# The shift of a DiT block's modulation, computed by four 128x32 column tiles of TensorE in place of 81 narrow matmuls

## The chip, the core and the metric

The kernel runs on one core of one Trainium2 chip. The metric is the device time of one execution in microseconds (us). "Before" is the kernel without the change, "after" the kernel with it. The engines are TensorE (PE; its weight loads, PEld, are listed apart), VectorE (DVE), ScalarE (ACT), GpSimd (POOL) and SyncE (SP), which issues most of the DMAs.

## The reference

The first half of a DiT block with adaptive layer norm: two samples of 256 tokens with 1152 features, one attention head over all features, all inputs in bf16.

```python
B, N, D = 2, 256, 1152
mod = (silu(c) @ w_mod).reshape(B, 6, 1, D)
shift_a, scale_a, gate_a, shift_m, scale_m, gate_m = [mod[:, i] for i in range(6)]
h = layernorm(x) * (1 + scale_a) + shift_a          # eps 1e-5, no affine
qkv = h @ wqkv
q, k, v = qkv[..., :D], qkv[..., D:2*D], qkv[..., 2*D:]
p = softmax(einsum('bqd,bkd->bqk', q, k) * D ** -0.5)
a = einsum('bqk,bkd->bqd', p, v) @ wo
return x + gate_a * a
```

Only the first three of the six parts of `mod` are used: the shift, the scale and the gate of the attention.

## The kernel before

The 512 tokens (T) of both samples lie side by side in the free dimension; the 1152 features are KT = 9 blocks of P = 128 partitions. x is normalised, turned so that features lie on the partitions (`xnT`), and multiplied by 1 + scale. Everything runs in one pass, in this order:

1. *Load.* SP issues the loads in a written order: x, the scale columns of w_mod (`wS`), K's columns of wqkv (`wK`), the shift columns of w_mod (`wH`, five DMAs), then Q's and V's columns in chunks of 384 (`wqv`), the gate columns (`wG`) and wo (`wO`). The rows of w_mod are dealt out so that partition p holds the rows 9p to 9p + 8; so one step kk of a product with w_mod takes one of the nine rows of every partition.
2. *K without the shift.* K is computed from `hTs`, the normalised tokens times 1 + scale, without the shift and before the 1/std of each token is applied. A shift of h adds to the scores of a query one number for all keys, which softmax drops. K's feature blocks 0 to 5 (`accs`) accumulate while x and the weights arrive; the first three k of blocks 6 and 7 are kept in `early`. What is left of blocks 6 and 7 (six matmuls each, k = 3 to 8) is computed later by `k_block` and added to `early` by VectorE; these are the two "early blocks". Block 8 (`k_block(8, ps, 0)`) is nine matmuls.
3. *1/std.* `rstd_bc`, the 1/std of each token on all partitions, is copied out of `spread_ps`, and VectorE multiplies it into the nine blocks of `xnT`.
4. *Shift.* `shift_block(kk)` accumulates the shift in `psH`: for each of the nine feature blocks j it loads the 128x128 block of `wH` as the stationary operand and lets silu(c) stream past it. silu(c) of the two samples is repeated 27 times to NR = 54 columns (`scT_rep`). So one step kk is nine weight loads and nine matmuls of 54 columns, and nine steps are 81. Four steps run before early block 6, one after it, four after early block 7. Then VectorE copies two of the 54 columns of each block to `sh`, a table of 128 partitions x 9 blocks x 2 samples.
5. *hT.* `modulated(i)` makes the full h from `xnT`, `s1p` (1 + scale) and `sh`, 18 instructions of 128x256: two of every three on VectorE, the third on ScalarE. K's block 8 runs on TensorE meanwhile.
6. *Q.* Nine feature blocks f, each nine matmuls over k of `hT` with 512 columns; ScalarE copies each block out to `qkT`.
7. *Scores, softmax, V, attention, output.* VectorE makes the gate in 18 steps (`gate_step`) between other work and GpSimd sums it over the partitions (`gate_bc`). The output projection, gate and residual end the kernel.

The order of each engine's instructions is the order in which the program issues them: helpers (`ten`, `vec`, `sca`, `gps`, `spq`) record every instruction, and `pin` ties each to the one before it on its engine. All of these instructions therefore carry one line in the profile, L74, and are told apart by the names of their tiles. PSUM has eight banks here: six in the pool `psum` (tag "mm"), one each in `psum_a` and `psum_b`. `evac(1, ...)` is a copy on ScalarE.

Of the kernel before, what the change touches and what calls it, by code (L numbers as in the profile page):

```python
# [10 lines left out]
F32 = mybir.dt.float32  # L11
# [5 lines left out]
def kernel(  # L17
# [10 lines left out]
    P = 128  # L28
    B, N, D = x.shape
    T = B * N  # L30
    KT = D // P
    TT = T // P
    NQ = N // P
    CW = 384
# [5 lines left out]
    NEARLY = 2  # L40
# [3 lines left out]
    NR = 54  # L44
# [7 lines left out]
    const = ctx.enter_context(tc.tile_pool(name="const", bufs=1))  # L52
# [4 lines left out]
    psum = ctx.enter_context(tc.tile_pool(name="psum", bufs=6, space=PSUM))  # L57
    psum_a = ctx.enter_context(tc.tile_pool(name="psum_a", bufs=1, space=PSUM))
# [22 lines left out]
    vec = _Rec(nc.vector, dve_seq)  # L81
    sca = _Rec(nc.scalar, act_seq)
    ten = _Rec(nc.tensor, pe_seq)
# [12 lines left out]
    def tok(b):  # L96
        return slice(b * N, (b + 1) * N)
# [4 lines left out]
        out=ident, in_=ident, compare_op=ALU.not_equal, fill=1.0, base=0,  # L102
# [14 lines left out]
        out=pick, in_=pick, compare_op=ALU.is_ge, fill=0.0, base=0,  # L117
# [3 lines left out]
        out=pick, in_=pick, compare_op=ALU.is_ge, fill=0.0, base=NT - 1,  # L121
# [12 lines left out]
    chunks_w = [wpool.tile([P, KT, CW], BF16, tag=f"wchunk{i}", name="wqv") for i in range(2 * NCH)]  # L134
    wmpool = ctx.enter_context(tc.tile_pool(name="wmpool", bufs=1))
    wS = wmpool.tile([P, KT, D], BF16, tag="wS")
    wH = wmpool.tile([P, KT, D], BF16, tag="wH")
# [63 lines left out]
    def sc_rhs(kk):  # L201
        return scT_rep[:, kk].rearrange("p r b -> p (r b)")
# [5 lines left out]
    hT = act.tile([P, KT, T], BF16)  # L208
# [62 lines left out]
    def rstd_spread():  # L271
        ps = psum_a.tile([P, TT, P], F32, tag="pa", name="spread_ps")
        for t in range(TT):
# [3 lines left out]


    s1p = const.tile([P, KT, B], F32)
    sh = const.tile([P, KT, B], F32)  # L280
    hTs = act.tile([P, KT, T], BF16, tag="a3")
    qkT = act.tile([P, 2 * KT, T], BF16)
    early = const.tile([P, NEARLY, T], F32)
# [3 lines left out]
               rhs=ones_row[0:1, 0 : (KA - 1) * NR], start=True, stop=False, skip_group_check=True)  # L287
    psS0 = psum_b.tile([P, NR], F32, tag="pb")
    ten.matmul(psS0, lhsT=ones_bf[0:1, :], rhs=ones_row[0:1, 0:NR], start=True, stop=False,
               skip_group_check=True)  # L290
# [19 lines left out]
            for b in range(B):  # L310
                scaled(k, tok(b), s1p[:, k, b : b + 1])

    def shift_block(kk):
        for j in range(KT):
            ten.matmul(
                psH[:, j, :], lhsT=wH[:, kk, j * P : (j + 1) * P], rhs=sc_rhs(kk),
                start=(kk == 0 and j == 0), stop=(kk == KT - 1), skip_group_check=True,
            )

    def one(t):  # L320
# [26 lines left out]
    def k_block(f, ps, k0):  # L347
        for k in range(k0, KT):
            ten.matmul(
                ps, lhsT=wK[:, k, f * P : (f + 1) * P], rhs=hTs[:, k, :],  # L350
                start=(k == k0), stop=(k == KT - 1),
            )

    def evac(idx, out_ap, in_ap):
        if idx % 2 == 0:
            return vec.tensor_copy(out=out_ap, in_=in_ap)
        return sca.copy(out=out_ap, in_=in_ap)
# [100 lines left out]
        k_step(k)  # L458
    for f in range(NACC):
        evac(1, qkT[:, KT + f, :], accs[f])  # L460
    psH = psum_a.tile([P, KT, NR], F32, tag="pa")
    for kk in range(4):
        shift_block(kk)
    for i in range(NEARLY):
        pool, tag = (psum_b, "pb") if i == 0 else (psum, "mm")
        ps = pool.tile([P, T], F32, tag=tag, name="ps")
        k_block(NACC + i, ps, KA)
        vec.tensor_tensor(out=qkT[:, KT + NACC + i, :], in0=ps, in1=early[:, i, :], op=ALU.add)
        shift_block(4 + i)
    for kk in range(4 + NEARLY, KT):  # L470
        shift_block(kk)
    vec.tensor_copy(out=sh, in_=psH[:, :, 0:B])
    for f in range(NACC + NEARLY, KT):
        ps = psum.tile([P, T], F32, tag="mm")
        k_block(f, ps, 0)
# [32 lines left out]
        spq.dma_start(out=wO[:, k0 : k0 + 3, :], in_=wo_v[:, k0 : k0 + 3, :])  # L508


    for f in range(KT):
        wt, off = chunks_w[f * P // CW], f * P % CW
        ps = psum.tile([P, T], F32, tag="mm")
        for k in range(KT):
            ten.matmul(
                ps, lhsT=wt[:, k, off : off + P], rhs=hT[:, k, :],
                start=(k == 0), stop=(k == KT - 1),
            )
        evac(1, qkT[:, f, :], ps)


    s_tiles = []
    for b in range(B):
        s_ps = psum.tile([P, NQ, N], F32, tag="mm")
        for i in range(NQ):
            tq = b * NQ + i
            for k in range(KT):
                ten.matmul(
                    s_ps[:, i, :],
                    lhsT=qkT[:, k, tq * P : (tq + 1) * P],  # L530
                    rhs=qkT[:, KT + k, tok(b)],
                    start=(k == 0), stop=(k == KT - 1),
# [96 lines left out]
    for b in range(B):  # L629
        for gi, dv0 in enumerate(range(0, KT, 2)):  # L630
            ndv = min(2, KT - dv0)
            ps = psum.tile([P, 2, N], F32, tag="mm")
            for dd in range(ndv):
                dv = dv0 + dd
                for j in range(NQ):
                    ten.matmul(
                        ps[:, dd, :], lhsT=v_sb[:, b * NQ + j, dv * P : (dv + 1) * P], rhs=pT_sbs[b][:, j, :],
                        start=(j == 0), stop=(j == NQ - 1),
# [3 lines left out]
    for t in range(TT):  # L642
# [9 lines left out]
        for ci, (c0, w_) in enumerate(chunks):  # L652
# [3 lines left out]
            ps = psum.tile([P, w_], F32, tag="mm")  # L656
            if pregated:
                ten.matmul(ps, lhsT=ident, rhs=x_sb[:, t, cs], start=True, stop=False)
            for k in range(KT):
                ten.matmul(  # L660
                    ps, lhsT=attnT[:, k, t * P : (t + 1) * P],
                    rhs=(wo_last[:, k, c0 - (D - TAILW) : c0 - (D - TAILW) + w_] if pregated else wO[:, k, cs]),
                    start=(k == 0 and not pregated), stop=(k == KT - 1),
# [50 lines left out]
```

## Time and profile before

| | us |
|---|---|
| median of 3 runs | 98.16 (97.86 to 98.18) |
| the profiled execution, whole | 97.95 |
| the profiled execution, span from its first to its last instruction | 96.2 |
| TensorE busy | 91.2 (95% of the span) |
| VectorE busy | 70.6 (73%) |
| ScalarE busy | 33.5 (35%) |
| GpSimd busy | 21.4 (22%) |
| mean granted clock of TensorE | 0.996 of full speed |
| bytes moved by DMA | 21.31 MB |

All other times are positions in the span or durations of that one execution. A row of the timeline gives the start, the length, the engine, the line, the operation, "out<-in" by the program's names, the shape and how many instructions were merged into the row. A row of the groups gives the busy time, the mean length of one instruction in ns, and the idle time of the engine before them with what ended it. A matmul row's length runs from its start to the modelled end of its results; matmuls overlap, so a stream advances faster than one instruction's length tells. In the chain of waits a piece is the time that the chain spent at this work.

### The profile page before, as it was taken

The page shows a single profiled execution, that of the slowest core. Times are in us where ns is not written, and L with a number is a line of the kernel's source. Part 1 is how long each engine was busy: PE and PEld are TensorE (multiplying, and loading weights), DVE is VectorE, ACT ScalarE, POOL GpSimd, SP SyncE. Part 2 cuts the span into 40 slices and gives each one's busy share as a digit, 9 for nine tenths or more (in the row PEclk, how much of TensorE's full clock was granted, in tenths as well). Part 3 has the DMA queues.
Part 4 walks back from the last instruction along what each step waited for, and adds up shares of the span by engine and source line. Part 5 has one row for each costly group of instructions (what it writes and reads, how often), then busy time and mean ns, then how long its engine had stood idle before and what let it go on. Part 6 is the DMA issues. An engine that isn't in the chain of part 4 may idle for free.

```text
span 96.2 us, 1804 instructions
## 1 busy us (share of the span) xinstructions
PE 91.2 (95%) x715; PEld 55.5 (58%) x720; DVE 70.6 (73%) x139; ACT 33.5 (35%) x67; POOL 21.4 (22%) x26
## 2 busy tenths in 40 slices
PE   5998899999999999999999999999999999999970
PEld 1338698454566444444458755665568755665760
DVE  0488589132999999999982999990229577999880
ACT  5297667202560962432231445331115400000010
POOL 6600000710000000000000000008999980007000
PEclk9999999999999999999999999999999999999998
DMA  2999999999999999999999502200000000303221
GB/s 47 303 350 344 348 391 375 396 395 407 395 380 400 383 407 393 373 371 372 383 410 410 220 2 55 50 5 0 0 0 0 7 0 0 123 1 122 98 97 51
DMA packets 19015, 21.31 MB, mean 222 GB/s; under 512 B 2752, under 2 KB 13632, under 8 KB 19008
## 3 DMA queue, kind: packets, MB, share of 16 engines
q1 hardware_dynamic: 18592, 21.16, 61.4%
q10 hardware_dynamic: 416, 0.05, 0.4%
q8 instruction: 5, 0.08, 0.3%
q14 instruction: 2, 0.02, 0.0%
HBM read 19.76 MB, written 1.18 MB: 218 GB/s over the span
## 4 chain that ended last, share of the span: by engine, by line
PE 85%; DMA 9%; DVE 1%; SPq 1%; issue 1%; ACT 0%
PE ps L74 63%; PE acc L74 12%; DMA x_sb<-in_x_dram 4%; DMA wK<-in_wqkv_dram 4%; PE s_ps L74 4%; PE psH L74 2%; PE psE L74 1%; PE tp L74 1%; SPq L74 1%; PE psL L74 1%; DVE xnT L74 0%; PE spread_ps L74 0%; ACT o_sb L74 0%; DVE hTs L74 0%; DVE o_sb L74 0%
## 5 line engine op out<-in xcount | busy, mean ns | idle before, releaser
L74 POOL PARTITION_ALL_REDUCE gate_bc<-gacc x2 | 13.7, 6886 | 45.5 <-DVE gacc L74 45.5
L74 DVE SCALAR_TENSOR_TENSOR gacc<-wG,scT_f,gacc 128x1152 f32<-128x1152 bf16 x16 | 22.7, 1418 | 0.5
L74 PE MATMUL ps<-wqv,hT 128*128 128x384 bf16 x108 | 17.7, 326 | 0.0
L74 PE MATMUL ps<-hT,wqv 128*128 128x512 bf16 x80 | 17.6, 379 | 0.1
L74 PE MATMUL ps<-wO,attnT 128*128 128x384 bf16 (+1 forms) x108 | 17.0, 319 | 0.0
L74 PEld LDWEIGHTS <-attnT 128*128 128x128 bf16 x117 | 11.3, 98 | 6.3
L74 PEld LDWEIGHTS <-hT 128*128 128x128 bf16 x108 | 10.6, 98 | 6.9
L74 PE MATMUL acc<-hTs,wK 128*128 128x128 bf16 (+2 forms) x88 | 13.3, 292 | 0.8 <-DVE hTs L74 0.3
L74 PEld LDWEIGHTS <-wK 128*128 128x128 bf16 x123 | 9.9, 97 | 6.5 <-DMA wK<-in_wqkv_dram 0.7
L74 PEld LDWEIGHTS <-wqv 128*128 128x128 bf16 x81 | 7.8, 97 | 9.6 <-DVE hT L74 0.4
L74 ACT CAST qkT<-ps 128x512 bf16<-128x512 f32 x10 | 5.8, 583 | 10.9 <-PE ps L74 10.9
L74 DVE TENSOR_TENSOR ga<-ps,gate_bc 128x384 f32<-128x384 f32 (+1 forms) x12 | 6.5, 538 | 2.4 <-PE ps L74 2.4
L74 ACT CAST v_sb<-ps 128x384 bf16<-128x384 f32 x10 | 4.7, 476 | 9.8 <-PE ps L74 9.8
L74 DVE TENSOR_TENSOR o_sb<-ga,x_sb 128x384 bf16<-128x384 f32 (+1 forms) x12 | 7.0, 585 | 0.4
L74 DVE TENSOR_TENSOR xnT<-xnT,rstd_bc 128x512 bf16<-128x512 bf16 x9 | 5.5, 685 | 1.8 <-ACT rstd_bc L74 1.8
L74 PE MATMUL junk_ps<-junk_rhs 128*128 128x512 bf16 x13 | 5.7, 627 | 1.1 <-DVE junk_rhs L74 1.1
L74 ACT CAST o_sb<-ps 128x128 bf16<-128x128 f32 x1 | 0.3, 265 | 17.3 <-PE ps L74 17.3
L74 DVE BATCH_NORM_STATS2 stats<-x_sb 128x6 f32<-128x384 bf16 x6 | 3.1, 552 | 2.5 <-DMA x_sb<-in_x_dram 2.5
L74 PE MATMUL ps<-hTs,wK 128*128 128x512 bf16 x19 | 4.7, 378 | 0.1
L74 DVE CAST attnT<-ps 128x512 bf16<-128x512 f32 (+1 forms) x6 | 3.5, 603 | 1.7 <-PE ps L74 1.7
L74 DVE COPY xnT<-tp 128x384 bf16<-128x384 bf16 (+2 forms) x7 | 2.2, 347 | 3.3 <-PE tp L74 3.3
L74 DVE CAST v_sb<-ps 128x384 bf16<-128x384 f32 x2 | 1.1, 558 | 4.6 <-PE ps L74 4.6
(84 smaller groups left out, 91.8 us busy)
## 6 DMA issues: line engine op xcount, KB each, us to landing
wqv<-in_wqkv_dram SPq DMA_DIRECT2D x5, 864.0 KB, 10.1
wG<-in_w_mod_dram SPq DMA_DIRECT2D x3, 864.0 KB, 9.6
wO<-in_wo_dram SPq DMA_DIRECT2D x3, 864.0 KB, 8.5
wH<-in_w_mod_dram SPq DMA_DIRECT2D x4, 576.0 KB, 7.8
wS<-in_w_mod_dram SPq DMA_DIRECT2D x6, 288.0 KB, 6.0
wK<-in_wqkv_dram SPq DMA_DIRECT2D x6, 288.0 KB, 6.2
x_sb<-in_x_dram SPq DMA_DIRECT2D x4, 288.0 KB, 3.8
wqv<-in_wqkv_dram SPq DMA_DIRECT2D x3, 288.0 KB, 9.0
```

The lines of the kernel that those rows point to most:

```text
L74: r = fn(*a, **k)
```

## The change

- `shift_rows(kk)` takes the place of `shift_block(kk)`. Now silu(c) is the stationary operand, its first 32 columns (16 repeats of the two samples), and the row kk of `wH` moves. The array is used as four column tiles of 128x32 (`tile_position=(0, 32 * j)`): tile j gets of each of the nine feature blocks the 32 columns 32j to 32j + 31, so 288 moving columns, and writes the PSUM partitions 32j to 32j + 31. One step is four weight loads of 32 columns and four matmuls of 288; nine steps are 36.
- In `psH` the shift now lies with samples on the partitions (32 rows for each tile, only two of them different) and features in the free dimension. One VectorE `transpose`, which turns each 32x32 block by itself, writes it to `sh`; `sh` grows to 128 x 9 x 32, and its first two columns of each block are read as before.
- All nine steps stand in one piece after the two early blocks of K, ahead of K's block 8.
- Q's feature blocks 0 and 1 are computed side by side: for each k one matmul of each, into two PSUM tiles, and the two copies after both. The other seven blocks are as before.

```diff
-    sh = const.tile([P, KT, B], F32)
+    sh = const.tile([P, KT, 32], F32)
...
-    def shift_block(kk):
-        for j in range(KT):
+    def shift_rows(kk):
+        w4 = wH[:, kk, :].rearrange("p (f j c) -> p f j c", j=4, c=32)
+        for j in range(4):
             ten.matmul(
-                psH[:, j, :], lhsT=wH[:, kk, j * P : (j + 1) * P], rhs=sc_rhs(kk),
-                start=(kk == 0 and j == 0), stop=(kk == KT - 1), skip_group_check=True,
+                psH[32 * j : 32 * (j + 1), :, :], lhsT=sc_rhs(kk)[:, 0:32], rhs=w4[:, :, j, :],
+                start=(kk == 0), stop=(kk == KT - 1), skip_group_check=True, tile_position=(0, 32 * j),
             )
...
-    psH = psum_a.tile([P, KT, NR], F32, tag="pa")
-    for kk in range(4):
-        shift_block(kk)
     for i in range(NEARLY):
         pool, tag = (psum_b, "pb") if i == 0 else (psum, "mm")
         ps = pool.tile([P, T], F32, tag=tag, name="ps")
         k_block(NACC + i, ps, KA)
         vec.tensor_tensor(out=qkT[:, KT + NACC + i, :], in0=ps, in1=early[:, i, :], op=ALU.add)
-        shift_block(4 + i)
-    for kk in range(4 + NEARLY, KT):
-        shift_block(kk)
-    vec.tensor_copy(out=sh, in_=psH[:, :, 0:B])
+    psH = psum_a.tile([P, KT, 32], F32, tag="pa")
+    for kk in range(KT):
+        shift_rows(kk)
+    vec.transpose(out=sh.rearrange("p f r -> p (f r)"), in_=psH.rearrange("p f r -> p (f r)"))
     for f in range(NACC + NEARLY, KT):
         ps = psum.tile([P, T], F32, tag="mm")
         k_block(f, ps, 0)
...
-    for f in range(KT):
-        wt, off = chunks_w[f * P // CW], f * P % CW
-        ps = psum.tile([P, T], F32, tag="mm")
+    for fs in ((0, 1), *((f,) for f in range(2, KT))):
+        pss = [psum.tile([P, T], F32, tag="mm", name="ps") for _ in fs]
         for k in range(KT):
-            ten.matmul(
-                ps, lhsT=wt[:, k, off : off + P], rhs=hT[:, k, :],
-                start=(k == 0), stop=(k == KT - 1),
-            )
-        evac(1, qkT[:, f, :], ps)
+            for f, ps in zip(fs, pss):
+                wt, off = chunks_w[f * P // CW], f * P % CW
+                ten.matmul(
+                    ps, lhsT=wt[:, k, off : off + P], rhs=hT[:, k, :],
+                    start=(k == 0), stop=(k == KT - 1),
+                )
+        for f, ps in zip(fs, pss):
+            evac(1, qkT[:, f, :], ps)
```

## The prediction

> **What bounds the kernel now.** I read the page first, its busy shares and slices, to see which engine sets the pace.
>
> ```profile
> PE 91.2 (95%) x715; PEld 55.5 (58%) x720; DVE 70.6 (73%) x139; ACT 33.5 (35%) x67; POOL 21.4 (22%) x26
> PE   5998899999999999999999999999999999999970
> PEclk9999999999999999999999999999999999999998
> ```
>
> TensorE (PE) is busy 95% of the 96.2 us span at its full granted clock, with no thin slice between the first and the last 5 us. What it no longer does there can shorten the run; what others do counts only where TensorE waits for it. Next the chain of waits, at the stretch that the change touches.
>
> ```profile
> 23.41 2.70 PE acc L74 x12
> 26.10 0.91 PE psH L74 x36
> 27.01 0.06 issue
> 27.07 1.24 PE ps L74 x5
> 28.31 0.23 PE psH L74 x9
> 28.53 1.29 PE ps L74 x6
> 29.83 0.91 PE psH L74 x36
> 30.74 0.21 PE ps L74
> 30.96 0.05 issue
> 31.01 10.74 PE ps L74 x49
> ```
>
> The chain stays on TensorE: the shift (psH) stands on it with 36 + 9 + 36 = 81 matmuls and 0.91 + 0.23 + 0.91 = 2.05 us, 25.3 ns each. Then the timeline of the two engines that meet here, TensorE and VectorE (DVE).
>
> ```profile
> 25.94 1.07 PE L74 MATMUL psH<-scT_rep,wH 128*128 128x54 bf16 x36
> 32.52 7.72 PE L74 MATMUL ps<-hT,wqv 128*128 128x512 bf16 x35
> ...
> 24.06 5.51 DVE L74 TENSOR_TENSOR xnT<-xnT,rstd_bc 128x512 bf16<-128x512 bf16 x9 [1.77 <-ACT rstd_bc L74]
> 29.49 1.28 DVE L74 TENSOR_TENSOR qkT<-ps,early 128x512 bf16<-128x512 f32 x2
> 30.78 0.18 DVE L74 COPY sh<-psH 128x18 f32<-128x18 f32 x1
> 30.99 3.17 DVE L74 TENSOR_SCALAR hT<-xnT,s1p,sh 128x256 bf16<-128x256 bf16 x12
> ```
>
> Two things are to be seen. From the first shift matmul (25.94) to Q's first (32.52) lie 6.58 us: 81 of the shift and 21 of K with 512 columns at 0.216 us each (35 in 7.72: (7.72 - 0.379)/34 = 0.216), 4.53 + 2.05. No wait of TensorE is left in it. And VectorE has no gap from 24.06 to 34.1: its copy of sh starts at 30.78 because VectorE comes free then, as the last shift matmul ends. So VectorE is the second bound, right behind the first.
>
> **The change, part by part.** The durations come from the groups of instructions:
>
> ```profile
> L74 DVE TENSOR_TENSOR ga<-ps,gate_bc 128x288 f32<-128x288 f32 x2 | 0.9, 458 | 0.2 <-PE ps L74 0.2
> L74 PE MATMUL ps<-wO,attnT 128*128 128x288 bf16 x18 | 2.4, 286 | 0.0
> L74 PEld LDWEIGHTS <-wH 128*128 128x128 bf16 x81 | 2.5, 96 | 0.7
> L74 PE MATMUL turn_ps<-ident,parts 128*12 128x128 bf16 x1 | 0.2, 222 | 0.0
> ```
>
> *Removed:* 81 weight loads and 81 matmuls of 54 columns: -2.05 us of TensorE.
>
> *Added on TensorE:* 9 x 4 = 36 matmuls with a 32-column stationary and 9 x 32 = 288 moving columns each. What a stream pays per matmul: 0.216 us at 512 columns, 0.109 at 256 (36 of s_ps in 4.09 us: (4.09 - 0.272)/35), so 0.42 ns per column and 0.122 us at 288. A narrow stationary is no cheaper by itself: turn_ps, with 12 columns, took 222 ns where 36 full transposes of the same length average 219. So the price hangs on whether the four tiles of a step run side by side, which no row of before shows. Ends: side by side 9 x 0.122 = 1.10 us; one after another 36 x 0.122 = 4.41 us. I take side by side: the four are given separate 32-column tiles and write separate partitions, so nothing in the data orders them, and TensorE already keeps some seven of the shift's matmuls in flight (each lasts 185 ns, one starts every 25). The floor that the same row gives, 36 x 25.3 = 0.91 us, is below 1.10.
>
> To this come two changes between full array and tiles. Ends: nothing, or each time TensorE empties and loads weights anew, 286 - 122 = 164 ns of matmul after its last column plus 96 ns, 0.26 us; twice 0.52. The Trainium skill (TensorEngine Tiling (Array Packing), Key Properties) says that a change of tiling mode drains TensorE, which speaks for the upper end; no row here shows it, and by it the stage would take 1.10 + 0.52 = 1.62 us. I take 0.4 for both, nearer to the upper end, since the 25 ns at which whole-array weights follow one another are the pace of a pipe that stays full. Stage: S = 1.50 us, between 1.10 and 1.62.
>
> *Moved:* all of the shift comes after K's two early blocks. TensorE runs these 12 matmuls from 25.94 to 28.53, the shift until 28.53 + S = 30.03, K's last block (9 x 0.216 = 1.94) until 31.97. From TensorE's side Q could start at 30.47 + S = 31.97, against 32.52. The early blocks move up by up to 1.1 us, yet their two additions on VectorE stay where they are, since the nine products of xnT hold it until 29.5. PSUM is free: acc's first copies on ScalarE begin at 25.06, spread_ps was read by 24.02. No DMA and no queue of SP or GpSimd moves. w_mod's last rows are issued at 19.86 and take 8.9 us, so they land at 28.8; the last step needs them at 28.53 + 8 x 0.122 + a drain, 29.5 or later. Cover 0.7 us; gone, each late microsecond is one on TensorE.
>
> *VectorE:* the copy of 18 elements (177 ns) becomes a transpose of 288 fp32 columns from PSUM. No row has that operation. Ends: 0.22 us (the shortest copy of a transposed block, 128x128 bf16, 220 ns) and 0.76 us (two passes at the 1.05 ns per column between the PSUM reads of 256 and 512 fp32 columns, 424 and 692 ns, over their 156 ns of fixed cost). I take the row with the same size, type and source, 458 ns. VectorE comes free at 30.78, long after the shift's end at 30.03 + 0.16; behind the transpose queue the 12 hT instructions. The transpose ends at 31.24, hT starts at 31.28, its first k (two instructions, 0.60 us) is there at 31.88, and Q's first matmul may start some 0.05 later: 31.93.
>
> So Q starts at the later of 31.93 (VectorE) and 31.97 (TensorE): 31.97, or 0.55 us earlier. VectorE caps the gain: S = 1.10 would take 0.95 us off TensorE, but TensorE would then wait from 31.57 to 31.93. The two bounds meet at S = 1.46.
>
> *Q side by side:* the same 18 matmuls in another order, no price of its own. It covers hT's pace: its last k is ready 3.17 us after hT's start, 31.28 + 3.17 = 34.45. One block alone would want it at 31.97 + 8 x 0.216 = 33.70 and stall 0.75 us; the pair reaches it at 31.97 + 16 x 0.216 = 35.43. In between too: k = 3 needs six of VectorE's instructions, 5 x 0.257 + 0.34 = 1.63 us, so 32.91; the pair is there at 33.27. The pair's copies on ScalarE both come at its end, 2 x 0.58 us, while f = 2 takes 1.94.
>
> *After that* nothing takes the gain back: wqv's third chunk, issued at 31.09, lands 11.2 us later at 42.3 and is wanted at 44.2 - 0.55; VectorE's gates begin 0.3 us later but it idles 2.0 us before p_f; GpSimd has gate_bc's second half at 78.9, wanted at 83.
>
> **Sum.** -0.55 us: the profiled execution's 97.95 us (span 96.2) becomes 97.40. The median of the runs shown is 98.16, 0.21 above the profiled one; from it, 97.6.
>
> **Rivals.** *Rounds do not overlap.* The Trainium skill (TensorE: Matmul & The Clock Gate, Part 3) states that weight loads overlap matmuls in flight only where the row groups differ; column tiles use all rows. In before's trace it does not hold for whole-array weights: wH's loads start at 25.73 while K's matmuls run, with none lost. Should it hold for tiles, a step's weights wait until the matmuls of the step before have ended: 9 x (0.286 + 0.096) = 3.44 us in place of 2.05. Place: between the steps of the shift. TensorE binds (30.47 + 3.44 = 33.91 against 32.52): +1.4, 99.55 us, slower. It decides against the change from S = 2.05, that is from 0.11 us of exposed time per step above 1.10. For it: each step accumulates on the same 32 partitions as the one before, with other weights. Against: so do all of before's steps of psH, at 25 ns. Chance 0.12.
>
> *Only the loads are exposed.* The tiles overlap, but each step adds a load of 96 ns: 1.10 + 0.86 = 1.96, and with the changes of mode 2.0 to 2.5: 98.1 to 98.6, taken 98.3. Chance 0.15, split between no change and slower.
>
> *The tiles run one after another* (the change doesn't do what it says): S = 4.41, Q at 34.88, +2.36, 100.5. For it: turn_ps, where unused columns buy nothing. Chance 0.14.
>
> *The transpose is dear:* at 0.76 us hT starts at 31.58, Q at 32.23: 97.9; at 1.05 us the gain is nil, 98.2. Against: no VectorE row of up to 300 columns takes half of that. Chance 0.05, nearly all of it no change.
>
> **How the numbers follow.** The forecast case has the other 0.54. With S from 1.10 to 1.62 and the transpose from 0.22 to 0.76, Q starts between 31.69 and 32.23, so its own range is 97.3 to 97.9. About 0.3% (0.3 us) is what a measurement of this kernel can tell from no change; the case is faster by more in 0.51 of all and within it in 0.03. Faster 0.51; no change 0.03 + 0.08 + 0.05 = 0.16; slower 0.12 + 0.07 + 0.14 = 0.33. The range runs from 97.3 to 99.6, over the rounds that do not overlap; left out are the serial tiles (0.14) and some 0.05 below.
>
> **What would show it.** Right: psH's 36 matmuls in fours starting within a few tens of ns and a new four every 0.12 us; 28.53 to about 30.0 for the stage; the transpose at 30.8 behind the two additions, near 0.46 us; Q's first matmul near 31.95 and no gap in the pair. Wrong: psH's matmuls evenly 0.12 us apart (serial), or fours 0.2 to 0.4 us apart (loads or rounds exposed); a transpose over 0.8 us; or TensorE waiting inside the pair for hT.

## The result: slower by 0.6%, and the profile after

| | before | after |
|---|---|---|
| median, 13 runs each | 98.03 us (97.31 to 98.60) | 98.51 us (98.20 to 99.14) |
| ratio to before | | 1.0059 (95% interval 1.0033 to 1.0086) |
| the profiled execution, whole; span | 97.95; 96.2 us | 98.55; 96.6 us |

A gain of 0.55 us was forecast; the change costs 0.5 us. Times below are compared as ratios with runs of the kernel before on the same chip; a ratio is estimated from the executions no more than 1.5% above the fastest of their kernel, so it need not equal the quotient of the two medians, which are over all executions. First the page of after: the engines, TensorE's slices, and the loading queue (packets, MB, its share of the DMA engines), with the queue's line on before's page behind it.

```profile
PE 90.3 (93%) x671; PEld 54.3 (56%) x675; DVE 70.6 (73%) x139; ACT 33.4 (35%) x67; POOL 21.6 (22%) x26
PE   5988999989999999996999999999999999999970
q1 hardware_dynamic: 18592, 21.16, 65.8%
```

```profile
q1 hardware_dynamic: 18592, 21.16, 61.4%
```

TensorE's busy time fell by 0.9 us, yet the slice at 43.5 to 45.9 us is down to 6 tenths, where before stands at 9. The queue moves the same 21.16 MB in the same 18592 packets but holds the DMA engines for 65.8% of the span in place of 61.4%. Now the timeline of the two engines at the place of the change, in after, and behind it the rows of Q and the scores in before:

```profile
25.97 2.75 PE L74 MATMUL ps<-hTs,wK 128*128 128x512 bf16 x12
28.66 1.38 PE L74 MATMUL psH<-wH,scT_rep 128*32 128x288 bf16 x36
29.97 2.12 PE L74 MATMUL ps<-hTs,wK 128*128 128x512 bf16 x8
31.98 11.81 PE L74 MATMUL ps<-hT,wqv 128*128 128x512 bf16 x53
44.58 6.00 PE L74 MATMUL ps<-hT,wqv 128*128 128x512 bf16 x27 [0.79 <-DMA wqv<-in_wqkv_dram]
50.41 4.09 PE L74 MATMUL s_ps<-qkT 128*128 128x256 bf16 x36
...
29.52 1.28 DVE L74 TENSOR_TENSOR qkT<-ps,early 128x512 bf16<-128x512 f32 x2
30.72 0.47 DVE L74 STREAM_TRANSPOSE sh<-psH 128x288 f32<-128x288 f32 x1
31.23 3.17 DVE L74 TENSOR_SCALAR hT<-xnT,s1p,sh 128x256 bf16<-128x256 bf16 x12
```

```profile
32.52 17.64 PE L74 MATMUL ps<-hT,wqv 128*128 128x512 bf16 x80
50.00 4.09 PE L74 MATMUL s_ps<-qkT 128*128 128x256 bf16 x36
```

All that was forecast at the place of the change came: the shift in 1.41 us (from 28.56, the slot after K's last early matmul, to 29.97), the transpose behind the two additions, Q's first matmul at 31.98 against 32.52 before. Then Q stops. Its seventh block would start at 31.98 + 54 x 0.216 = 43.64 and starts at 44.58, waiting for its weights: 0.94 us lost for 0.54 gained. The scores begin at 50.41, 0.41 later than before's 50.00, and it stays so to the end. The chain of waits tells where the weights were:

```profile
27.61 3.57 SPq L74
31.18 0.04 issue
31.23 0.85 SPq L74
32.08 0.04 issue
32.12 12.41 DMA wqv<-in_wqkv_dram
44.53 0.05 issue
44.58 6.00 PE ps L74 x27
```

Before's chain stays on TensorE here; this one goes over SP's queue and the load of wqv's third chunk. That was issued at 31.09 and took 11.2 us before (landing at 42.3); it is issued at 32.12 and takes 12.4 now. Both are late: the loads ahead of it in the queue run slower too. The rate itself stands in the windows (length of the stretch, clock, share of the DMA engines, GB/s), first of before, then of after:

```profile
25.00:45.00 20.00, 1.00 1.07 386
```

```profile
25.00:45.00 20.00, 1.00 1.08 357
```

The engines are equally full and move 7.5% less. The new work is not needed for it: from 5 to 25 us, where both kernels still run the same instructions (until 25.9), the windows give 378 and 362 GB/s. This early stretch tells less than the later one, since kernels whose loads are not slow later on have from 350 to 380 GB/s in it.

### The profile page after: what moved, and what is told of

Read it like the earlier page. It is cut to its first block, busy times and chain, and to the rows that moved or that the text cites. A ratio compares the mean times of both kernels' runs of the same rounds, so it can differ in the third digit from the quotient of the medians.

```text
span 96.6 us, 1715 instructions
## 1 busy us (share of the span) xinstructions
PE 90.3 (93%) x671; PEld 54.3 (56%) x675; DVE 70.6 (73%) x139; ACT 33.4 (35%) x67; POOL 21.6 (22%) x26
## 3 DMA queue, kind: packets, MB, share of 16 engines
q1 hardware_dynamic: 18592, 21.16, 65.8%
## 4 chain that ended last, share of the span: by engine, by line
PE 57%; DMA 30%; SPq 8%; issue 1%; ACT 0%; DVE 0%
PE ps L74 47%; DMA wS<-in_w_mod_dram 18%; DMA wqv<-in_wqkv_dram 13%; SPq L74 8%; PE acc L74 5%; PE s_ps L74 4%; PE psL L74 0%; PE spread_ps L74 0%; ACT o_sb L74 0%; DVE o_sb L74 0%; PE turn_ps L74 0%
## 5 line engine op out<-in xcount | busy, mean ns | idle before, releaser
L74 ACT CAST qkT<-ps 128x512 bf16<-128x512 f32 x10 | 5.7, 583 | 11.2 <-PE ps L74 11.2
L74 PE MATMUL junk_ps<-junk_rhs 128*128 128x512 bf16 x13 | 5.0, 568 | 1.1 <-DVE junk_rhs L74 1.1
L74 DVE TENSOR_SCALAR hTs<-xnT,s1p 128x256 bf16<-128x256 bf16 (+1 forms) x20 | 4.2, 273 | 0.1
```

Source lines behind the costliest of these rows:

```text
L74: r = fn(*a, **k)
```

## The experiments

The diff has one line that the prediction passed over: `sh` grows from 72 to 1152 bytes per partition. Pools lay their tiles one behind the other, so the addresses in the built programs differ from there on. They are bytes in each partition, read from the programs and not from a trace; the steps between them fit the sizes of the tiles (wK: 39936 + 9 x 1152 x 2 = 60672).

```
tile           before   after   difference   after, beyond a multiple of 256
sh              23072   23072
wK              39936   40992      1056      32
wqv (first)     60672   61728      1056      32
x_sb           102144  103200      1056      32
wS, wG         183808  184864      1056      32
wH, wO         204544  205600      1056      32
```

Before, every tile in the list below sh starts on a multiple of 256; after, none does. Three theories follow: A, the layout slows the loads; B, the new work does (four streams at once, or Q meeting loads that were late anyhow); C, the load rate is chance.

| kernel | median, us | before beside it | ratio (95% interval) | q1's share of the DMA engines |
|---|---|---|---|---|
| before_grown | 98.52 | 97.97 | 1.0053 (1.0021 to 1.0085) | 65.2% |
| before_padded | 98.10 | 97.97 | 0.9993 (0.9963 to 1.0023) | 61.7% |
| after_padded_256 | 97.52 | 97.97 | 0.9947 (0.9917 to 0.9978) | 62.0% |
| after_padded_64 | 98.57 | 97.97 | 1.0070 (1.0040 to 1.0099) | 65.6% |
| after_padded_128 (one execution) | 98.34 | 97.99 | | 65.6% |
| before_again (one execution) | 97.83 | 97.99 | | 61.7% |
| after_q_chunk_first | 97.64 | 97.86 | 0.9988 (0.9951 to 1.0026) | 66.5% |
| padded_q_single | 97.90 | 98.02 | 1.0012 (0.9982 to 1.0042) | 61.4% |
| padded_shift_narrow | 98.31 | 98.02 | 1.0042 (1.0007 to 1.0077) | 61.6% |
| padded_shift_split | 97.56 | 98.02 | 0.9965 (0.9929 to 1.0001) | 61.5% |
| padded_add_late | 97.22 | 98.02 | 0.9915 (0.9881 to 0.9949) | 61.9% |
| padded_add_late_2 | 97.17 | 97.86 | 0.9895 (0.9862 to 0.9929) | 62.0% |

**The layout alone: before_grown and before_padded.**

```diff
# before_grown, against before
-    sh = const.tile([P, KT, B], F32)
+    sh = const.tile([P, KT, 32], F32)
-    vec.tensor_copy(out=sh, in_=psH[:, :, 0:B])
+    vec.tensor_copy(out=sh[:, :, 0:B], in_=psH[:, :, 0:B])
# before_padded: the copy as above, and
+    sh_room = const.tile([P, KT * 32 + 56], F32)
+    sh = sh_room[:, 0 : KT * 32].rearrange("p (f r) -> p f r", r=32)
```

> The kernel before with the table sh grown from 9x2 to 9x32 as in the change, and nothing else: the same 81 shift matmuls, the same copy of two columns. In SBUF everything allocated behind sh, all tiles that the loads write among it, moves up by 1056 bytes and so starts 32 bytes past a multiple of 64 and of 256, where before it started on one. Theory A (the layout): the loads become slower, about 355 GB/s from 25 to 45 us in place of 390, and the time rises to 98.4 to 98.9 us with no change in the work. Theory B (the new work: four moving streams, or Q reaching its weights before they land): 98.0 us, as before, loads near 390 GB/s. Theory C (the load rate of one execution is chance): 98.0 us, any rate.

> The same with 224 bytes more behind sh, so that everything behind it moves by 1280 = 5 x 256 bytes and the loads' targets start on multiples of 256 again. Theory A: 98.0 us and loads near 390 GB/s, as before; if it came out as the kernel with the grown table alone, growth would matter and not where the tiles start. Theories B and C: 98.0 us.

The grown table makes the kernel before as slow as the kernel after, 98.52 and 98.51 us; 224 bytes of padding, which make the table larger still, give the time back. The loading queue on the page of before_grown, and its window:

```profile
q1 hardware_dynamic: 18592, 21.16, 65.2%
```

```profile
25.00:45.00 20.00, 1.00 1.08 357
```

The rate is that of after without a single tiled matmul, so B is out as the cause of the slow loads. In before_padded the window reads:

```profile
25.00:45.00 20.00, 1.00 1.06 379
```

C is unlikely by the ratios (1.0053 against 0.9993) and gets a run of its own below. (The profiled executions of before_grown, 99.52 us, and before_padded, 98.77 us, are among their longest; the medians are used for their times.)

**The change on a good layout: after_padded_256, after_padded_64, after_padded_128.**

```diff
# against after; 56 gives + 1280 bytes (5 x 256), 8 gives + 1088, 24 gives + 1152
-    sh = const.tile([P, KT, 32], F32)
+    sh_room = const.tile([P, KT * 32 + 56], F32)
+    sh = sh_room[:, 0 : KT * 32].rearrange("p (f r) -> p f r", r=32)
```

> The kernel after with 224 bytes more behind sh (everything behind it 1280 bytes higher than before, on multiples of 256). Theory A: loads near 390 GB/s, no wait of TensorE for wqv, and the gain of the shift comes through: 97.4 to 97.6 us, 0.55 below before. Theory B: 98.5 us as after, with the wait for wqv's third chunk. Theory C: 98.5 us, since the slowdown would have another cause.

> The kernel after with 32 bytes more behind sh (everything behind it 1088 bytes higher than before: multiples of 64, but 64 bytes past a multiple of 256). Theory A with steps of 64 bytes deciding: as with the 256-byte padding, 97.4 to 97.6 us. Theory A with steps of 256 bytes deciding (the Trainium skill, DMA: Bandwidth & Descriptors, How a descriptor splits into AXI transactions, states that a transfer starting off a 256-byte boundary takes an extra transaction): as after, 98.3 to 98.6 us at 355 GB/s. Theories B and C: 98.5 us.

> The kernel after with 96 bytes more behind sh: everything behind it 1152 bytes higher than before, on multiples of 128 but not of 256. If multiples of 256 are what counts: the loads' share of the DMA engines near 65% as in after (before and the 256-byte paddings: 61.4 to 62.0%), some 357 GB/s from 25 to 45 us, and a wait for wqv. If 128 is enough: 62%, 385 GB/s, no wait.

With the 256-byte padding the change brings what was forecast: 97.52 us, 0.45 below the kernel before beside it. TensorE's timeline of after_padded_256 has no hole:

```profile
25.80 2.75 PE L74 MATMUL ps<-hTs,wK 128*128 128x512 bf16 x12
28.48 1.29 PE L74 MATMUL psH<-wH,scT_rep 128*32 128x288 bf16 x36
29.70 2.12 PE L74 MATMUL ps<-hTs,wK 128*128 128x512 bf16 x8
31.80 17.64 PE L74 MATMUL ps<-hT,wqv 128*128 128x512 bf16 x80
49.28 4.09 PE L74 MATMUL s_ps<-qkT 128*128 128x256 bf16 x36
```

From K's early blocks to Q it takes 31.80 - 25.80 = 6.00 us, against 6.58 before, and Q's 80 recorded matmuls run through. The windows give 387 GB/s. Multiples of 64 and of 128 do not help (of the second there is one execution); the waits of after_padded_128 are those of after:

```profile
PEld L74 <- DMA wqv<-in_wqkv_dram: 1.3, 1, 1.3
PE ps L74 <- DMA wqv<-in_wqkv_dram: 0.8, 1, 0.8
```

So it is multiples of 256 bytes that count. The Trainium skill (DMA: Bandwidth & Descriptors, How a descriptor splits into AXI transactions) states that a transaction has to start at a multiple of 256 bytes, so that a transfer which does not start on one begins at the boundary below it and pays for bytes that it does not use. Every run here agrees with the boundary, although the page speaks of bytes read and here it is the side written to, SBUF, that was moved. By that rule a row of 768 bytes (a chunk of wqv) 32 bytes off makes 4 transactions in place of 3 and 25 beats of 32 bytes in place of 24, and a row of 2304 bytes (wG, wO) 10 in place of 9 and 73 in place of 72; these are estimates. The one transaction more comes from the rows' being multiples of 256 bytes here; the rule does not give it for every transfer.

The share of the DMA engines times the span is the time for which they were held: 59.1 us in before, 63.6 in after, 63.5 in after_padded_64 and 63.2 in after_padded_128. The growth of some 7% lies between what beats and what transactions would give. Counted in beats, a larger offset would be dearer (28 in place of 24 for 768 bytes at 128 off, an estimate by the same rule), and the runs show no such growth; the one transaction more, the same for 32, 64 and 128 off, fits that better. Why it costs what it does stays open. Every run moved all tiles behind sh together. That it is the targets of the loads that matter, and not some other tile, is argued from the DMA rate; VectorE's busy time is 70.4 us in before_grown against 70.6 in before, so nothing shows on that engine.

**Is the rate chance? before_again.** The kernel before, unchanged.

> The kernel before, unchanged, for a second profile: if the load rate goes with the layout, its loads take 61 to 62% of the DMA engines and run near 385 GB/s from 25 to 45 us; if it is chance from one execution to the next, any value from 355 on.

61.7% of the DMA engines and 387 GB/s: the nine kernels profiled on multiples of 256 hold the engines 61.4 to 62.0% of the span (58.9 to 59.8 us), the five others 65.2 to 66.5% (63.2 to 63.7 us), with nothing in between. The rate goes with the layout.

**Is it this one load? after_q_chunk_first.**

```diff
# against after
-        if i == 1:
+        if i == 2:
             load_mod(wG, 2, 3, 6, 0, D)
             load_mod(wG, 2, 6, KT, 0, D)
```

> The kernel after as it is (targets 32 bytes past a multiple of 64, slow loads), with wqv's third chunk loaded ahead of the second and third part of wG instead of behind them. If the wait for that chunk is all that takes the gain away: no wait for wqv at Q's block 6, Q ends 0.8 us or more earlier, 97.5 to 97.7 us with loads still at 357 GB/s and 65% of the DMA engines; the gates on VectorE wait for wG instead, some 2.4 us longer, off the path. If slow loads cost elsewhere too (the start of the kernel, K's weights): 97.9 to 98.3 us.

The loads stay slow, but the wait is gone: Q runs through, and the time falls from a ratio of 1.0059 to 0.9988. The gates pay, on VectorE:

```profile
31.87 17.65 PE L74 MATMUL ps<-hT,wqv 128*128 128x512 bf16 x80
...
42.34 8.69 DVE L74 SCALAR_TENSOR_TENSOR gacc<-wG,scT_f,gacc 128x1152 f32<-128x1152 bf16 x6 [3.91 <-DMA wG<-in_w_mod_dram]
```

The scores begin at 49.36 us, against 50.41 in after and 49.28 in after_padded_256. That confirms the wait for the third chunk as the place where the gain went. The padded kernel is at 0.9947; what slow loads and later gates cost beyond that wait is within the intervals and stays open. One part of it is in the trace: w_mod's last rows land at 29.64 us here, the last step of the shift starts at 29.68 in place of 29.36, and Q begins 0.17 us later than in after_padded_256, counted from K's twelve `acc` matmuls before the early blocks (31.87 - 23.10 against 31.80 - 23.20). This kernel's chain ends on VectorE (its last addition starts at 92.66 us), and its last gate step starts at 66.1 us, 2.0 later than in after; that the one follows from the other is not shown.

**The parts of the change, on the padded layout.** Three kernels each undo or bend one part of after_padded_256: Q's first blocks one after the other; the 81 narrow matmuls in the new place; the tiled steps in three pieces of 4, 1 and 4.

```diff
# padded_q_single
-    for fs in ((0, 1), *((f,) for f in range(2, KT))):
+    for fs in ((f,) for f in range(KT)):
# padded_shift_narrow: shift_block of the kernel before in place of shift_rows, and
-    vec.transpose(...)
+    vec.tensor_copy(out=sh[:, :, 0:B], in_=psH[:, :, 0:B])
# padded_shift_split: psH made ahead of the early blocks, then
+    for kk in range(4):
+        shift_rows(kk)
     for i in range(NEARLY):
...
+        shift_rows(4 + i)
+    for kk in range(4 + NEARLY, KT):
+        shift_rows(kk)
```

> The kernel after with the 256-byte padding, and Q's blocks 0 and 1 one after the other as before. If the pair is what covers hT's pace: block 0 waits for hT, its ninth matmul starts near 34.3 us (hT from 31.05, 3.17 us long) instead of 31.80 + 8 x 0.216 = 33.5; 0.7 to 0.8 us lost, 98.2 to 98.3 us. Rival (the pair does nothing): 97.5 us, no wait.

> The kernel after with the 256-byte padding, its shift computed by the 81 matmuls of 54 columns again, in the new place, with the copy of two columns in place of the transpose. If the tiles are what gains: the stage takes 2.05 us instead of 1.3, Q starts near 32.4 instead of 31.80, 98.0 to 98.1 us. If the move and the pair gain by themselves: 97.5 to 97.7 us.

> The kernel after with the 256-byte padding, the nine tiled steps in three pieces of 4, 1 and 4 as the narrow ones stood before: six changes between full array and tiles instead of two. If a change costs about 0.1 us (the stage's 1.31 us less 1.10 of moving columns, over two): 0.4 us more on TensorE, of which 0.15 fills its wait for hT: 97.7 to 97.8 us. If a change costs 0.26 (the upper end in the prediction): 1.0 us more, 98.3 to 98.4. If it costs nothing and the 0.2 us is the start of the stage's first weights: 97.5 us.

*padded_q_single* is at a ratio of 1.0012 against 0.9947, and the intervals do not overlap: 0.0065, some 0.64 us. Its median, 97.90 us, is lower than the 98.2 to 98.3 expected, 0.12 below the kernel before beside it, so whether all of the gain or the larger part of it is lost stays open. Its profiled execution (99.36 us) was late from before 26 us on, so only the stage is read, and the waits of TensorE's weight loads for hT:

```profile
33.03 18.40 PE L74 MATMUL ps<-hT,wqv 128*128 128x512 bf16 x80
51.27 4.09 PE L74 MATMUL s_ps<-qkT 128*128 128x256 bf16 x36
```

```profile
PEld L74 <- DVE hT L74: 1.8, 5, 0.7
```

Q takes 51.27 - 33.03 = 18.24 us up to the scores, against 49.28 - 31.80 = 17.48 with the pair, where no wait for hT is listed. 0.76 us: the pair is needed. (The kernel before takes 50.00 - 32.52 = 17.48 without a pair: its Q starts 1.53 us behind hT's first instruction, not 0.75.)

*padded_shift_narrow*:

```profile
25.44 2.75 PE L74 MATMUL ps<-hTs,wK 128*128 128x512 bf16 x12
28.03 2.22 PE L74 MATMUL psH<-scT_rep,wH 128*128 128x54 bf16 x81
30.09 2.10 PE L74 MATMUL ps<-hTs,wK 128*128 128x512 bf16 x8
32.03 17.64 PE L74 MATMUL ps<-hT,wqv 128*128 128x512 bf16 x80
```

The stage is back at 2.06 us (28.03 to 30.09) and Q starts 6.59 us after the early blocks' start, as before (6.58). The median is 0.2 us above what was expected, which its profile (97.66 us) does not explain. That the tiles gain, and not the move or the pair by themselves, is clear either way: 0.59 us in the trace.

*padded_shift_split*:

```profile
25.90 0.68 PE L74 MATMUL psH<-wH,scT_rep 128*32 128x288 bf16 x16
26.51 1.47 PE L74 MATMUL ps<-hTs,wK 128*128 128x512 bf16 x6
27.91 0.31 PE L74 MATMUL psH<-wH,scT_rep 128*32 128x288 bf16 x4
28.15 1.25 PE L74 MATMUL ps<-hTs,wK 128*128 128x512 bf16 x5
29.55 0.67 PE L74 MATMUL psH<-wH,scT_rep 128*32 128x288 bf16 x16
30.15 2.12 PE L74 MATMUL ps<-hTs,wK 128*128 128x512 bf16 x9
```

From the first tiled matmul to the next full one go 0.61, 0.24 and 0.60 us, where 4, 1 and 4 steps of 0.122 us are 0.49, 0.12 and 0.49: leaving the tiles costs 0.11 to 0.12 us. Entering costs 0.10: six matmuls from 26.51 end their slots at 27.81, the tiles start at 27.91. So a visit costs 0.22 us, in agreement with 1.31 = 1.10 + 0.21 for the single visit. What that time consists of (emptying the array, loading the first weights) the rows do not tell. Q starts at 32.10, 0.29 us later than in after_padded_256 when both are counted from K's `acc` matmuls (23.21 here, 23.20 there). The median, 97.56 us, lies below the 97.7 to 97.8 expected; by the ratios 0.18 us is lost, well within the intervals, so the price rests on the trace.

**Does VectorE hold Q back? padded_add_late, twice.** In after_padded_256, K's block 8 leaves TensorE free at 29.70 + 9 x 0.216 = 31.65, and Q starts at 31.80.

```diff
# against after_padded_256: the addition for i = 1 moves behind the 18 hT instructions
+        early_ps.append(ps)
+        if i == 0:
+            add_early(i)
...
     for i in range(KT * B):
         modulated(i)
+    add_early(1)
```

> The kernel after with the 256-byte padding, and VectorE's second addition of early moved behind the 12 hT instructions. Theory that VectorE holds Q back (in the padded kernel TensorE could start Q at 31.65 us and starts at 31.80, behind hT's first two instructions): the transpose starts as the shift ends, near 29.9 instead of 30.54, Q follows K's block 8 without a gap, 0.15 us gained over the padded kernel: 97.3 to 97.4 us. Rival (the gap comes from the change of tiling, not from hT): the same time as the padded kernel, 97.5 us, and the gap stays.

> The kernel with the 256-byte padding and the late addition once more, beside the run above, as the quickest version so far: 97.2 to 97.4 us.

```profile
29.65 2.12 PE L74 MATMUL ps<-hTs,wK 128*128 128x512 bf16 x8
31.60 17.65 PE L74 MATMUL ps<-hT,wqv 128*128 128x512 bf16 x80
...
29.90 0.47 DVE L74 STREAM_TRANSPOSE sh_room<-psH 128x288 f32<-128x288 f32 x1
30.40 3.17 DVE L74 TENSOR_SCALAR hT<-xnT,s1p,sh_room 128x256 bf16<-128x256 bf16 x12
```

Counted from K's early blocks (25.75 here, 25.80 in after_padded_256, where the transpose starts at 30.54) the transpose starts 0.59 us earlier and Q 0.15, without a gap behind K's block (29.65 + 1.94 = 31.59). The gap was VectorE's. At 97.22 and 97.17 us, ratios 0.9915 and 0.9895, this version beats both kernels. The medians fell below after_padded_256 by more than the 0.15 us of the trace, and a little below what was expected (97.3 and 97.2 us at least), but both intervals overlap that of after_padded_256.

## Why the prediction was wrong

*The step that failed* is "After that nothing takes the gain back", together with the sentence "No DMA and no queue of SP or GpSimd moves" under "Moved". The order of the queue does not move, but the targets do. The prediction took the landing of wqv's third chunk from before's row, 42.3 us, and set it against a need at 44.2 - 0.55 = 43.65; it landed at 44.53, because the loads ran slower (357 GB/s in place of 386 from 25 to 45 us). The cover of 0.7 us for w_mod's last rows was cut in the same way: in after_padded_64 the last step of the shift waits for them, with TensorE idle for 0.16 us. The first line of the diff, the grown table, was given no price at all, and none of the rivals contained it: the slower outcome came by none of the three mechanisms that were priced for it. That 98.51 us still lies inside the stated range is luck, since the range reached up to 99.6 only for a rival, rounds that do not overlap, which did not occur.

As the chunk's landing sets when Q can go on, an earlier start of Q gains nothing: with slow loads the kernel takes 98.5 us with the old shift (before_grown) and with the new one. In the trace of before_grown Q stops at the same block, which starts at 45.73 in place of 33.24 + 54 x 0.216 = 44.90; but that execution was late from its start, so it does not show that this wait is all that the old shift loses.

*What was right*, by its own steps. The tiles run side by side: the timeline of after from 28.6 to 28.9 us has eight of them, two steps, within 0.43 us, each lasting 0.29.

```profile
28.66 0.43 PE L74 MATMUL psH<-wH,scT_rep 128*32 128x288 bf16 x8
```

That takes out the serial rival (0.12 us from one to the next) and the two with exposed loads or rounds: a step follows the last in 0.12 us, although its four weight loads share all rows with the matmuls in flight. So the rule behind the rival "Rounds do not overlap" does not hold in this case. The stage was put at 1.50 us and took 1.31 on the good layout (1.41 in after, where the loads were slow); what was too dear is the change between array and tiles, 0.4 for two against 0.21. The transpose was put at 458 ns and took 471. Q's start was put at 31.97 and came at 31.98, and that they agree so well is luck, since small errors cancel: K's block left TensorE free at 29.97 + 9 x 0.216 = 31.91, and Q followed hT's first start (31.23, put at 31.28) by 0.75 us, not 0.65. So VectorE was the bound, if by little, and taking one addition off its path moved Q by 0.15 us on the good layout. The pair was put at 0.75 us of cover and is worth 0.76. The sum of -0.55 us came as -0.45 us by the medians of after_padded_256; its interval, 0.9917 to 0.9978 of before, is -0.8 to -0.2 us and holds the sum.

## What to carry to other kernels

A tile that grows moves every tile allocated behind it: before a change is priced, list the addresses that loads write to before and after, and keep them on multiples of 256 bytes. Where the loads fill the DMA engines for half the run, as here to some 54 us in before and 57 in after, the slack of each landing is part of the price of any gain on TensorE, since 7.5% of load rate moved this landing by 2.2 us. A gain that vanishes although every step of it is seen in the trace is looked for at the first wait for a load behind it, and in the share of the DMA engines on the first page.

## What was not expected of the hardware

- Load targets off a multiple of 256 bytes in SBUF: 357 to 359 GB/s from 25 to 45 us and 65.2 to 66.5% of the DMA engines, against 379 to 388 GB/s and 61.4 to 62.0%, for the same packets and bytes. 32, 64 and 128 bytes off cost the same.
- Four 128x32 column tiles with 288 moving columns take one step in 0.122 us, the price worked out for one such matmul; entering and leaving the tiles costs 0.10 and 0.11 to 0.12 us.
